# Diagonal sums of five groups by TensorE, loads limited by bytes, and a new order of instructions

## The chip, the cores and the metric

The kernel runs on one core of a Trainium2 chip. Its time is that of one execution on the device in microseconds (us). Five engines work side by side, each through its own queue in the order in which the program gives it instructions: TensorE (PE, with its weight loads as PEld), VectorE (DVE), ScalarE (ACT), GpSimd (POOL) and SyncE (SP). DMAs are issued by SP and at the beginning by ACT; q1 is SP's DMA queue, q8 brings instructions.

## The reference

A linear attention with a decayed state feeds a gated feed-forward layer. Shapes are B=4, H=8 heads, S=768 steps, D=48; x has 384 features, the hidden layer 1024.

```python
for t in range(S):
    kt, vt, rt = k[:, :, t], v[:, :, t], r[:, :, t]
    cur = einsum('bhd,bhe->bhde', u * kt, vt)
    y[:, :, t] = einsum('bhd,bhde->bhe', rt, state + cur)
    state = w * state + einsum('bhd,bhe->bhde', kt, vt)
x = y.transpose(0, 2, 1, 3).reshape(B, S, H * D)
h = maximum(x @ w_in, 0)
conv = conv_w[0] * h[t - 1] + conv_w[1] * h[t] + conv_w[2] * h[t + 1]
out = (h * sigmoid(conv)) @ w_out
```

The current step enters y with u in place of the state: its share is (sum over d of r·u·k) times v, a sum on the diagonal of the score matrix.

## The kernel before, in words

**Attention.** Time is cut into 24 groups of 128 steps (six for each batch row), each of two chunks of 64. A group's data lie in four rotating buffers: KR (k and r with features on the partitions, two DMAs for the two halves of the partitions), and TOK (k, r and v with time on the partitions; `ldT` is its load of k and r, `ldV` that of v). `prep(g)` readies group g: VectorE multiplies KR by powers of the decay (`KR`), GpSimd scales k by tokens (`KS`), and the diagonal of the scores is made. For the first `NE` = 2 groups this diagonal comes from a product k·r with features on the partitions (`P`), 16 TensorE products with one column each (`pq`), and a VectorE multiply with an identity (`dg`); for all others from token products on GpSimd (`KRT`, `KRU`), a reduction on VectorE (`QQ`) and the diagonal on GpSimd (`dg`, in `diagonal`). From group `GP` = 5 on a ScalarE copy (`TKc`) puts the powers into the scores' bank before the multiply.

`visit(g)` is one TensorE stretch: the outputs of group g (bank AV), and the scores (bank SP, key "SUs") and state update (bank UP) of group g+1. Behind it a VectorE copy under a mask (`msk`) adds the scores to the diagonal of group g+1 in SC, and the state goes forward by a multiply (`M`, MM) and an addition (`SA`, SS). For group 2 a visit is cut in two (outputs, then scores). Visit -1 makes only group 0's scores. The outputs go to XF (first three groups) or XT (split into two fp32r parts), and small DMAs (`mv`) move rows of x between partitions.

**Feed-forward.** x is worked through in seven units of columns with eight blocks f of hidden features each. `first` (f1) makes one block in HP0 or HP1, followed by relu, convolution, sigmoid and product in ACT and DVE (HP, CV) and, from unit 1 on, a split into two parts (`GH`, `GL`); `second` (f2) adds up the output in PO0 to PO2. Unit 0 works in fp32. The weights come in 16 pieces of 384 KB; `convert` unpacks a piece with two ACT steps and a DVE step into WF, and `split` makes its two fp32r parts, the high one on ACT and the low one on DVE or POOL.

**The order** of the instructions on all engines comes from the class `Plan`: each step has a cost and a due time, a list of random changes to the due times (`MOVES`: a seed, a share, a size, a place in time) shifts them, and `order` picks at each point the earliest possible and most urgent step. Where it believes TensorE idle ahead of the first f2 it adds a product of 512 columns into PO0 that nobody reads, a fill. Loads of the classes in `LONG` wait for earlier ones: no more than `LOADS` = 6 in flight, and `LATER` = 4 after the first `FIRST` = 40. The loads of groups 4 to 7 also wait for a gate, the mask copy of the group two before.

```python
lim = min(max(f, ready[i]) for i in av) + DELTA
i = min((late[i] - (BON if e == "pe" and ops[i][5] == mode else 0.0), i) for i in av if ready[i] <= lim)[1]
```

## Time and profile before

| | us |
|---|---|
| median of three runs | 302.86 |
| lowest, highest | 302.4, 304.26 |
| the profiled execution | 304.27 |
| its span in the trace | 302.5 |
| TensorE busy | 287.7 (95%) |
| VectorE busy | 222.5 (74%) |
| ScalarE busy | 176.4 (58%) |
| GpSimd busy | 166.2 (55%) |

The span runs from the first to the last instruction of the trace; the execution's own time holds what lies around it. Busy shares are means over the whole span. A visit shows in the trace as lines L638 (scores), L647 and L654 (outputs) and L651 (state); L641 and L644 belong to group 2 alone. f1 is L741, f2 is L788 in unit 0 and L791 later; L874 is a fill. L373 is the helper `tt` for all tensor products on DVE and POOL, which are told apart by their tiles.

### The profile page before, as it was taken

To read this page: it belongs to the slowest core of one execution; us is meant where nothing else is said; L and a number is where in the kernel's file an instruction comes from. 1 tells how busy PE (TensorE), PEld (TensorE's weight loads), DVE (VectorE), ACT (ScalarE), POOL (GpSimd) and SP (SyncE) were. 2 spreads that over 40 slices of the span, in tenths; PEclk is the share of its full clock that TensorE was granted. 3 is DMA by queue.
4 is the path that set the end of the run, shared out by engine and by line. 5 is a ranking of instruction groups with operands and counts; after the bars stand their busy time and mean duration, and the time that the engine had idled before them with its cause. 6 is when DMAs were issued, how large, how long until landed. Compare 5 with 4: busy or idle time off the path is not lost.

```text
span 302.5 us, 9831 instructions
## 1 busy us (share of the span) xinstructions
PE 287.7 (95%) x4104; PEld 239.2 (79%) x4110; DVE 222.5 (74%) x359; ACT 176.4 (58%) x348; POOL 166.2 (55%) x196
## 2 busy tenths in 40 slices
PE   7979999869998999999999999999999999999994
PEld 2657666546777888889888888888888988899993
DVE  5766579896998876877879984899867755556561
ACT  3135484857776456664656753667735665556663
POOL 8367686984678884787735846658511111131230
PEclk9997999998999999999999999999999999999999
DMA  6994695855655535646424453554210020001102
GB/s 155 226 240 130 201 278 158 243 166 158 187 176 154 148 106 146 178 119 172 141 75 126 114 179 64 133 139 143 75 49 14 15 96 7 9 0 62 33 0 78
DMA packets 24011, 37.00 MB, mean 122 GB/s; under 512 B 6256, under 2 KB 16784, under 8 KB 23968
## 3 DMA queue, kind: packets, MB, share of 16 engines
q1 hardware_dynamic: 23632, 36.04, 42.7%
q8 instruction: 32, 0.52, 0.7%
q10 hardware_dynamic: 336, 0.35, 0.5%
q14 instruction: 11, 0.09, 0.1%
HBM read 29.49 MB, written 4.72 MB: 113 GB/s over the span
## 4 chain that ended last, share of the span: by engine, by line
PE 67%; DMA 6%; DVE 5%; POOL 4%; issue 3%; SPq 2%; ACT 2%; POOLq 0%; DVEq 0%; ACTq 0%
PE HP L741 29%; PE PO L791 25%; PE SP L638 4%; POOL TOK L373 3%; PE AV L654 3%; PE PO L788 3%; DMA TOK<-in_krt_dram 2%; PE AV L647 2%; SPq L382 2%; PE UP L651 2%; DMA KR<-in_krd_dram 1%; DMA ST<-in_w_in_dram 1%; DVE CV L753 1%; DVE KR L373 1%; DMA XF<-XF 1%
## 5 line engine op out<-in xcount | busy, mean ns | idle before, releaser
L741 PE MATMUL HP<-XT,wi 128*128 128x464 f32 (+2 forms) x432 | 98.8, 373 | 0.2 <-DVE CV L757 0.2
L791 PE MATMUL PO<-GG,wo 128*128 128x462 f32 (+2 forms) x432 | 97.5, 369 | 0.7 <-POOL GG L763 0.7
L753 DVE SCALAR_TENSOR_TENSOR CV<-HP,cw,CV 128x462 f32<-128x462 f32 (+2 forms) x112 | 75.2, 672 | 21.2 <-ACT CV L750 19.9
L791 PEld LDWEIGHTS PO<-GG,wo 128*128 128x128 f32 x432 | 80.2, 189 | 9.7 <-POOL GG L763 0.9
L741 PEld LDWEIGHTS HP<-XT,wi 128*128 128x128 f32 x432 | 79.5, 189 | 9.6 <-issue 0.4
L763 POOL TENSOR_TENSOR GG<-CV,GG 128x462 fp32r<-128x462 f32 (+2 forms) x30 | 34.7, 1156 | 65.6 <-ACT GG L762 61.0
L749 ACT ACTIVATE HP<-HP 128x464 f32<-128x464 f32 (+2 forms) x56 | 29.3, 523 | 50.4 <-PE HP L741 50.3
L638 PE MATMUL SP<-KR 48*64 48x64 f32 x768 | 46.3, 233 | 5.6 <-DVE KR L373 4.1
L757 DVE TENSOR_TENSOR CV<-HP,CV 128x462 f32<-128x462 f32 (+2 forms) x56 | 34.3, 612 | 21.3 <-ACT CV L756 21.0
L638 PEld LDWEIGHTS SP<-KR 48*64 48x64 f32 x768 | 38.9, 137 | 12.2 <-DVE KR L373 5.9
L654 PE MATMUL AV<-SC,TOK 64*48 64x64 f32 x760 | 47.0, 223 | 0.0
L647 PE MATMUL AV<-KR,SS 48*48 48x64 f32 x696 | 43.8, 223 | 0.0
L756 ACT ACTIVATE CV<-CV 128x462 f32<-128x462 f32 (+2 forms) x56 | 31.9, 569 | 19.8 <-DVE CV L753 19.6
L651 PE MATMUL UP<-TOK 64*48 64x48 f32 x704 | 41.3, 209 | 2.2 <-DVE SS L373 2.2
L750 ACT ACTIVATE CV<-HP,cw 128x462 f32<-128x462 f32 (+2 forms) x56 | 35.1, 627 | 2.3 <-ACT HP L749 0.4
L651 PEld LDWEIGHTS UP<-TOK 64*48 64x48 f32 x704 | 34.1, 127 | 2.3 <-DVE SS L373 2.3
L654 PEld LDWEIGHTS AV<-SC,TOK 64*48 64x48 f32 x760 | 35.7, 124 | 0.0
L647 PEld LDWEIGHTS AV<-KR,SS 48*48 48x48 f32 x696 | 32.5, 123 | 2.0 <-issue 2.0
L373 POOL TENSOR_TENSOR SC<-eye,QQ 128x512 f32<-128x512 f32 x22 | 23.4, 1064 | 18.0 <-PE AV L654 14.2
L762 ACT CAST GG<-CV 128x462 fp32r<-128x462 f32 (+2 forms) x48 | 27.2, 566 | 9.5 <-DVE CV L757 9.1
L373 POOL TENSOR_TENSOR TOK<-TOK 128x384 f32<-128x384 f32 x22 | 22.6, 1027 | 17.9 <-DMA TOK<-in_krt_dram 17.9
L373 POOL TENSOR_TENSOR MM<-SS,w 112x192 f32<-112x192 f32 x36 | 19.0, 528 | 17.1 <-DVE SS L373 15.7
(85 smaller groups left out, 358.8 us busy)
## 6 DMA issues: line engine op xcount, KB each, us to landing
KR<-in_krd_dram SPq DMA_DIRECT2D x46, 192.0 KB, 4.1
TOK<-in_krt_dram SPq DMA_DIRECT2D x22, 384.0 KB, 4.4
TOK<-in_vt_dram SPq DMA_DIRECT2D x47, 96.0 KB, 3.5
ST<-in_w_in_dram SPq DMA_DIRECT2D x8, 384.0 KB, 3.8
ST<-in_w_out_dram SPq DMA_DIRECT2D x8, 384.0 KB, 3.8
XT<-XT SPq DMA_DIRECT2D x126, 16.0 KB, 2.0
...
```

Of the source, the lines that this page charges most:

```text
L373: op(eng, d, rd, wr, lambda e: e.tensor_tensor(**kw), cls, port=not psum)
L638: PE.matmul(SP_[xs[x], p, c], KK[j][rows[x], p, t], RR[j][rows[x], p, t], start=True, stop=True)
L647: PE.matmul(outs[x], state(2 * g + c)[rows[x], p], RR[i][rows[x], p, t], start=not direct, stop=False)
L651: PE.matmul(UP[rows[x], n:n + D], TOK[j][xs[x], 0, p, c], TOK[j][xs[x], 2, p, c], start=True, stop=True)
L654: PE.matmul(outs[x], TOK[i][xs[x], 2, p, c], SC[g % 2][xs[x], p, c], start=none and not direct, stop=True)
L741: PE.matmul(hp[:, at:at + n_], WF[f][:, 0, j * 128:j * 128 + 128] if full else wi[a][:, j, fs], XF[:, j, c0:c0 + w] if full else src(x, j, y),
L750: op("act", act(n, 0, 1), [H_, "cw"], [("T", ti)], lambda e: A.activation(t1, hp[:, 1:n + 1], AF.Copy, scale=cw[:, 3 * f + 1:3 * f + 2]), ...
L753: op("dve", dve(n, psum=1) + 0.02, [H_, "cw"], [("T", ti)], lambda e, k=k: V.scalar_tensor_tensor(out=t1, in0=hp[:, k:n + k], scalar=cw[:, ...
L756: op("act", act(n, 1), [], [("T", ti)], lambda e: A.activation(t1, t1, AF.Sigmoid), "SG")
L757: op("dve", dve(n), [H_], [("T", ti)], lambda e: V.tensor_tensor(out=t1, in0=hp[:, 1:n + 1], in1=t1, op=ALU.mult), "GG")
L763: op("any", {"dve": dve(n), "pool": pool(n, "GL")}, [("T", ti), ("GH", gi)], [("GL", gi)], lambda e: e.tensor_tensor(out=gg(gi)[:, 1, :n], ...
L791: PE.matmul(po[:, :n], wo[a][:, f, ms], gg(gi)[:, x, :n], start=f == 0 and j == 0, stop=f == NF - 1 and j == 2)
```

## The change

Five groups instead of two (`NE`) take their diagonal from TensorE. `pq` is written anew: the product k·r moves through the array (128 columns for each head), and the factor u·w is the stationary operand, spread over 64 columns, so the sum comes out already repeated in 64 rows. That makes eight products instead of 16, and an output of a whole bank. Groups 0 to 2 use HP0, HP1 and PO1; groups 3 and 4 use the scores' bank SP itself. `pks` (scaled k of group 0) moves to PO1. The diagonal step of these groups is the VectorE multiply, and `P` of groups 2 to 4 may go to VectorE or GpSimd. The load of r by tokens for groups 2 to 4 falls away. Loads are no longer counted: their sizes (1.3 for 384 KB of TOK, 0.63 for a half of KR, 0.3 for one of v, 1.28 for a weight piece) may add up to `WAY` = 6.0 in flight. The planner's model of loading code changes, and `MOVES` has a new list of numbers, so everything is in another order.

```diff
-LONG, LOADS = ('ldK', 'ldT', 'ldV', 'wdma'), 6
-NE = 2
+LONG, WAY = ('ldK', 'ldT', 'ldV', 'wdma'), 6.0
+NE = 5
...
-FBASE, FETCH, FIRST, LATER = 3.4, 0.7, 40, 4
+FBASE, FETCH = 3.4, 0.8
...
 MOVES = [
-    (982228, 0.4, 3.0, 105.0), (679522, 0.004, 3.0, 75.0), (769013, 0.03, 1.0, 105.0), (831907, 0.03, 3.0, 45.0),
...
+    (5566, 0.1, 3.0, 105.0), (905251, 0.03, 1.0, 60.0), (855037, 0.1, 8.0, 45.0), (191337, 0.4, 3.0, 0.0),
...
                 if cls in LONG:
-                    k = LOADS if len(loads) < FIRST else LATER
-                    if len(loads) >= k:
-                        tc.add_manual_dep(i.ins, loads[-k].ins.name, behind_, reason="loads")
-                    loads.append(i)
+                    k, way = len(loads), x
+                    while k and way <= WAY:
+                        k -= 1
+                        way += loads[k][1]
+                    if way > WAY:
+                        tc.add_manual_dep(i.ins, loads[k][0].ins.name, behind_, reason="loads")
+                    loads.append((i, x))
...
         def bank(g):
-            return [(HP[0], ("HP", 0)), (HP[1], ("HP", 1)), (PO[1], ("PO", 1))][g] if g < 3 else (UP, "UPq")
+            return [(HP[0], ("HP", 0)), (HP[1], ("HP", 1)), (PO[1], ("PO", 1))][g] if g < 3 else (SP_.rearrange("q p c t -> q (p c t)"), "SUs")
...
-                tt("dve" if g < 3 else ANY, 512, kr(i), [("SC", g % 2)], "P", out=pp, in0=KK[i][0:112], in1=RR[i][0:112], op=ALU.mult)
+                tt("dve" if g < 2 else "any", 512, kr(i), [("SC", g % 2)], "P", out=pp, in0=KK[i][0:112], in1=RR[i][0:112], op=ALU.mult)
...
                 def mq(e):
-                    for c in range(2):
-                        for p in range(NP):
-                            for x in range(2):
-                                r = slice(64 * x, 64 * x + D)
-                                n = NP * 2 * D + p * 2 + c
-                                PE.matmul(kb[64 * x:64 * x + C, n:n + 1], s[r, p, c], uw[r, p:p + 1], start=True, stop=True)
+                    for p in range(NP):
+                        for x in range(2):
+                            r = slice(64 * x, 64 * x + D)
+                            PE.matmul(kb[64 * x:64 * x + C, p * GT:(p + 1) * GT], uw[r, p:p + 1].broadcast_to([D, C]), s[r, p].rearrange("q c t -> q (c t)"), start=True, stop=True)
...
-                op("pe", 1.1, [("SC", g % 2), "uw"], [key], mq, "pq", 1200, mode=1, k=32)
-                q = kb[:, NP * 2 * D:NP * 2 * D + H]
-                if g < 3:
-                    op("dve", dve(512, psum=1), [key, "eye"], [("SC", g % 2)], lambda e: V.tensor_tensor(
-                        out=s.rearrange("q p c t -> q (p c) t"), in0=eye.unsqueeze(1).broadcast_to([128, 2 * NP, C]), in1=q.unsqueeze(2).broadcast_to([128, 2 * NP, C]), op=ALU.mult), "dg")
-                    return
-                op("act", 0.2, [key], [("QQ", g % 2)], lambda e: A.copy(QQ[g % 2], q), "qc")
-                diagonal(g)
+                op("pe", 0.95, [("SC", g % 2), "uw"], [key], mq, "pq", 2100, mode=1, k=16)
+                op("dve", dve(512, psum=1), [key, "eye"], [("SC", g % 2)], lambda e: V.tensor_tensor(
+                    out=s.rearrange("q p c t -> q (p c) t"), in0=eye.unsqueeze(1).broadcast_to([128, 2 * NP, C]), in1=kb.rearrange("q (n t) -> q n t", t=C), op=ALU.mult), "dg")
                 return
```

The order moves at three places of which the prediction speaks. The first is TensorE's queue ahead of visit 3, which begins with the scores of group 4 (KR0_61) and the outputs of group 3 (KR3_64); before:

```order
L874 LDWEIGHTS wz_102
L874 MATMUL PO0_127<-wz_102 128x512
L741 MATMUL HP0_125<-XF_80,WF0_89 128x384 x3
L741 MATMUL HP1_126<-XF_80,WF1_90 128x384 x3
L638 MATMUL SP_122<-KR0_61 64x64 x2
L647 MATMUL AV_124<-KR3_64,SS2_73 48x64 x2
L651 MATMUL UP_123<-TOK0_65 48x48 x2
L654 MATMUL AV_124<-SC1_70,TOK3_68 48x64 x2
```

and now, from the end of visit 2 on (L664 is its last state product, L591 the products for the diagonal of group 4):

```order
L664 MATMUL UP_123<-TOK3_68 48x48 x2
L754 MATMUL HP0_125<-XF_80,WF0_89 128x384 x3
L754 MATMUL HP1_126<-XF_80,WF1_90 128x384 x3
L591 MATMUL SP_122<-SC0_69,uw_106 64x128 x8
L651 MATMUL SP_122<-KR0_61 64x64 x2
L660 MATMUL AV_124<-KR3_64,SS2_73 48x64 x2
L664 MATMUL UP_123<-TOK0_65 48x48 x2
L667 MATMUL AV_124<-SC1_70,TOK3_68 48x64 x2
```

The fills ahead of the first f1 are gone, and eight products into the scores' bank stand between the second f1 and visit 3.

The second is VectorE around visit 1, which needs the state additions SS3 and SS0. Before (KR3_64 is group 3, L659 a mask copy, L509 a weight or convolution piece):

```order
L509 SCALAR_TENSOR_TENSOR WF0_89<-ST1_100 128x384
L373 TENSOR_TENSOR SS3_74<-MM0_75,UP_123 112x192
L659 COPY_PREDICATED SC1_70<-mask_107,SP_122 128x512
L373 TENSOR_TENSOR KR3_64<-KR3_64,PO2_129 112x1024
L373 TENSOR_TENSOR SS0_71<-MM1_76,UP_123 112x192
L509 SCALAR_TENSOR_TENSOR ST0_99<-ST0_99 128x24
L509 SCALAR_TENSOR_TENSOR WF1_90<-ST2_101 128x384
```

and now (L672 is the mask copy, L528 a piece, L598 the diagonal of group 2):

```order
L528 SCALAR_TENSOR_TENSOR ST0_99<-ST0_99 128x24
L672 COPY_PREDICATED SC1_70<-mask_107,SP_122 128x512
L389 TENSOR_TENSOR SS3_74<-MM0_75,UP_123 112x192
L389 TENSOR_TENSOR MM1_76<-SS3_74,w64_112 112x192
L528 SCALAR_TENSOR_TENSOR WF1_90<-ST2_101 128x384
L389 TENSOR_TENSOR SS0_71<-MM1_76,UP_123 112x192
L598 TENSOR_TENSOR SC0_69<-eye_109,PO1_128 128x512
L389 TENSOR_TENSOR KR3_64<-KR3_64,PO2_129 112x1024
L389 TENSOR_TENSOR wi1_118<-WF1_90,wi0_117 128x3x128
L672 COPY_PREDICATED SC0_69<-mask_107,SP_122 128x512
```

The addition SS0 stood behind group 3's multiply and stands now ahead of it, behind the second w_in piece (WF1); the low half of that piece (wi1) comes ahead of group 2's mask.

The third is VectorE ahead of visit 6, which needs group 7 (KR3_64 again). Before:

```order
L753 SCALAR_TENSOR_TENSOR CV4_88<-HP0_125,cw_121,CV4_88 128x382
L659 COPY_PREDICATED SC0_69<-mask_107,SP_122 128x512
L509 SCALAR_TENSOR_TENSOR WF6_95<-ST2_101 128x384
L373 TENSOR_TENSOR SS2_73<-MM1_76,UP_123 112x192
L373 TENSOR_TENSOR KR3_64<-KR3_64,SP_122 112x1024
L757 TENSOR_TENSOR CV4_88<-HP0_125,CV4_88 128x382
```

and now:

```order
L672 COPY_PREDICATED SC0_69<-mask_107,SP_122 128x512
L389 TENSOR_TENSOR XT_79<-AV_124,XT_79 112x4x128
L389 TENSOR_TENSOR SS2_73<-MM1_76,UP_123 112x192
L389 TENSOR_TENSOR KR3_64<-KR3_64,SP_122 112x1024
L766 SCALAR_TENSOR_TENSOR CV4_88<-HP0_125,cw_121,CV4_88 128x382
L528 SCALAR_TENSOR_TENSOR WF6_95<-ST2_101 128x384
```

The piece WF6 stood ahead of the addition and the multiply and stands now behind them.

## Rows read from the trace of the kernel before

**Rows 1.** Windows by stage: length, busy us (instructions), granted clock, DMA share, GB/s.

```profile
23.00:26.40 3.40, 3.17 (x120) 3.17 (x120) 2.00 (x3) 2.14 (x6) 2.43 (x3) 0.52 0.28 83
28.40:33.00 4.60, 4.59 (x161) 4.50 (x162) 1.38 (x3) 2.10 (x6) 2.22 (x4) 1.00 0.64 200
67.40:70.80 3.40, 3.40 (x66) 2.39 (x58) 3.04 (x5) 1.89 (x4) 2.55 (x3) 0.52 0.71 202
92.60:94.10 1.50, 0.02 (x1) 0.00 (x0) 0.74 (x2) 0.59 (x1) 1.50 (x2) 1.00 0.61 204
94.20:292.50 198.30, 198.11 (x2591) 176.99 (x2591) 146.37 (x233) 119.44 (x223) 98.01 (x106) 1.00 0.33 92
```

**Rows 2.** Timeline of PE: start, duration, instruction, idle time before and releaser.

```profile
16.13 0.25 PE L638 MATMUL SP<-KR 48*64 48x64 f32 x2
...
18.23 2.54 PE L874 MATMUL PO<-wz 128*128 128x512 bf16 x11 [0.16 <-issue]
...
23.23 0.32 PE L651 MATMUL UP<-TOK 64*48 64x48 f32 x2 [2.21 <-DVE SS L373]
...
35.52 4.04 PE L741 MATMUL HP<-XF,WF 128*128 128x384 f32 x12
39.49 0.27 PE L638 MATMUL SP<-KR 48*64 48x64 f32 x2
...
46.53 0.27 PE L638 MATMUL SP<-KR 48*64 48x64 f32 x2 [0.39 <-DVE KR L373]
...
57.54 0.28 PE L638 MATMUL SP<-KR 48*64 48x64 f32 x2 [1.03 <-DVE KR L373]
...
66.31 0.33 PE L638 MATMUL SP<-KR 48*64 48x64 f32 x4 [2.66 <-DVE KR L373]
```

**Rows 3.** Timeline of DVE: product, diagonal, multiply of group 3, addition behind it.

```profile
8.30 0.69 DVE L373 TENSOR_TENSOR SC<-KR 112x512 f32<-112x512 f32 x1
...
10.80 0.68 DVE L582 TENSOR_TENSOR SC<-eye,HP 128x512 f32<-128x512 f32 x1
...
21.69 1.22 DVE L373 TENSOR_TENSOR KR<-KR,PO 112x1024 f32<-112x1024 f32 x1 [1.08 <-DMA KR<-in_krd_dram]
22.83 0.35 DVE L373 TENSOR_TENSOR SS<-MM,UP 112x192 f32<-112x192 f32 x1
```

**Rows 4.** The chain of waits, 27 to 36 us: start, us, what.

```profile
30.89 4.16 DMA KR<-in_krd_dram
```

**Rows 5.** Timeline of DVE, 56 to 66 us.

```profile
56.26 1.22 DVE L373 TENSOR_TENSOR KR<-KR,SP 112x1024 f32<-112x1024 f32 x1 [1.06 <-ACT SP L551]
57.40 0.55 DVE L509 SCALAR_TENSOR_TENSOR WF<-ST 128x384 int32<-128x384 int32 x1
...
62.19 2.67 DVE L509 SCALAR_TENSOR_TENSOR WF<-ST 128x384 int32<-128x384 int32 x1
```

**Rows 6.** Timeline of PE: the one-column products, then visit 2's products.

```profile
9.17 1.09 PE L573 MATMUL HP<-uw,SC 48*64 48x1 f32 x32
...
28.61 0.28 PE L644 MATMUL AV<-KR,SZ 48*64 48x64 f32 x4
28.73 0.28 PE L647 MATMUL AV<-KR,SS 48*48 48x64 f32 x4
```

**Rows 7.** Timeline of POOL: scaled k of group 1, diagonal of group 4, token product.

```profile
14.29 0.99 POOL L373 TENSOR_TENSOR TOK<-TOK,TH 128x384 f32<-128x384 f32 x1 [0.70 <-ACT TH L486]
...
41.30 1.04 POOL L373 TENSOR_TENSOR SC<-eye,QQ 128x512 f32<-128x512 f32 x1
...
62.50 0.99 POOL L373 TENSOR_TENSOR TOK<-TOK,TH 128x384 f32<-128x384 f32 x1
```

**Rows 8.** Timeline of ACT: a step of a weight piece.

```profile
23.35 0.55 ACT L504 ACTIVATE ST<-ST 128x384 f32<-128x384 f32 x1
```

**Rows 9.** Timeline of SP: the last move into XF.

```profile
31.52 0.51 SPq L382 DMA_DIRECT2D XF<-XF  x1
```

**Rows 10.** DMA issues, 0 to 75 us: count, KB each, median us to landing.

```profile
XF<-XF SPq DMA_DIRECT2D x3, 16.0 KB, 4.1
```

More of the change, by code (lines that the diff above doesn't have):

```diff
@@ L61 @@
 FN, FE, FW = 512, 6000, 3.4
-FBASE, FETCH, FIRST, LATER = 3.4, 0.7, 40, 4
+FBASE, FETCH = 3.4, 0.8
 GATED = 4
+DIRECT, ACTQ = (2,), (1,)
 DIRECT, ACTQ = (2,), (1,)
@@ L190, in fetched @@
                 at_ = max(s, s + (len(there) - 0.4 - a) * d, there[-1])
-                there.append(at_ + FBASE + FETCH * sum(1 for z in large[-8:] if z > at_))
+                there.append(at_ + FBASE + FETCH * max(0.0, dq - at_ - 0.9))
             for b in range(1, len(there)):
@@ L276, in order @@
                 if cls in LONG:
-                    large.append(done)
+                    large.append((done, x))
             else:
@@ L385, in issue @@
                 if cls in LONG:
-                    k = LOADS if len(loads) < FIRST else LATER
-                    if len(loads) >= k:
-                        tc.add_manual_dep(i.ins, loads[-k].ins.name, behind_, reason="loads")
-                    loads.append(i)
+                    k, way = len(loads), x
+                    while k and way <= WAY:
+                        k -= 1
+                        way += loads[k][1]
+                    if way > WAY:
+                        tc.add_manual_dep(i.ins, loads[k][0].ins.name, behind_, reason="loads")
+                    loads.append((i, x))
             op(q, dur, rd, wr, issue, cls, x, dma=True, gate=gate)
@@ L574, in prep @@
                 if g < NK:
-                    op("pe", 1.1, [k for k in kr(i) if k[0] == "KK"] + ["D64"], [key], mm, "pks", 1700, mode=1, k=32)
-                    op("act", act(384), [key], [("tK", i)], lambda e: A.copy(k_t.rearrange("q p c d -> q (p c d)"), kb[:, 0:NP * 2 * D]), "KSc")
+                    op("pe", 1.1, [k for k in kr(i) if k[0] == "KK"] + ["D64"], [kkey], mm, "pks", 1700, mode=1, k=32)
+                    op("act", act(384), [kkey], [("tK", i)], lambda e: A.copy(k_t.rearrange("q p c d -> q (p c d)"), ks[:, 0:NP * 2 * D]), "KSc")
```

10 lines of the change are left out of this document (7 added, 3 removed), and 49 rows, old and new, of the table MOVES.

## The prediction

> **What bounds the kernel now.** First I read the page's busy time: TensorE is busy for 287.7 of 302.5 us (the table above). The windows by stage say where the rest is [rows 1]: from 94.2 to 292.5 us TensorE is busy for 198.11 of 198.30 us at the full granted clock, so a us won before 94 is a us won at the end, and in that stretch a faster VectorE or GpSimd wins nothing. All that can be won lies ahead, and there it has three forms. TensorE runs fills, products into a bank that nobody reads (52 in the program; eleven took 2.54 us, 0.23 each [rows 2]); it stands still (2.21 us inside visit 1, 0.39, 1.03 and 2.66 us before visits 4, 5 and 6, each put down to VectorE [rows 2], and 1.5 us at 92.6 with no releaser [rows 1]); and twice the granted clock falls to half, 0.52 over 23.0 to 26.4 and over 67.4 to 70.8 us, just behind the two longest stops [rows 1]. A full TensorE loses 3.4 x (1 - 0.52) = 1.6 us in each.
>
> Then I followed each stop to its cause. Visit 1 waits for a state addition that stands on VectorE behind the multiply of group 3; this multiply waited 1.08 us for its load, and the addition ran only at 22.83 [rows 3]. Visit 3 starts at 39.49 [rows 2] behind the chain load of KR for group 4 (landed 30.89 + 4.16 = 35.05 [rows 4]), multiply, and GpSimd's token products. Visit 6 waits because a VectorE conversion, normally 0.55 us, took 2.67 us [rows 5] beside two GpSimd products, the first at 62.50 [rows 7], with the addition and the multiply of group 7 queued behind it.
>
> **The change part by part.** *The products.* Groups 0 and 1 had 16 one-column products, 1.09 us [rows 6]. Now groups 0 to 4 have eight of 128 columns. The trace of before has none; in visit 2 each set of two products of 64 columns on both row halves starts 0.12 us after the last one [rows 6], so 128 columns are 0.24 and four such sets 0.95 us. That lies near the 1.09 of the same helper, and I take 0.95; if the halves don't overlap it is 1.9. Groups 0 and 1 win 0.1 each; groups 2, 3 and 4 add 0.95 each. For 2 and 3 they replace fills (the program has 28 instead of 52) and cost nothing; for group 4 they stand bare between the second f1 and visit 3.
>
> *Diagonals.* Off GpSimd go two token products of 1.0 us and one diagonal of 1.04 us for each of groups 2, 3 and 4 [rows 7], 9.1 us in all; off VectorE goes the reduction. Added are a product on VectorE (0.69) or GpSimd (between 1.04 and 1.33, its 1.00 for 384 columns scaled to 512) and a VectorE diagonal of 0.68 [rows 3]. For groups 3 and 4 the products land in the scores' bank: the mask of the group before must have read it, and visit 3's score products wait until the diagonal of group 4 is out. That is a new stop of 0.68 plus two hand-overs, 0.9 us; VectorE's next item there is free to go, TensorE's queue holds visit 3 and everything behind it, and nothing hides it.
>
> *Loads.* Groups 2 to 4 load only k by tokens, 192 KB less each. Both orders move 3,640 KB up to the end of group 3's KR, so this multiply comes no earlier; what is gained is one more w_in piece among them and, up to group 4's last piece, 576 KB. The limit changes from six (later four) loads in flight to 6.0 units, some 1.8 MB; in the opening the queue is full either way, later loads wait for free buffers first.
>
> *The order, walked with the durations of before.* Visit 0 waited for the one-column products; now these come before the TH products, so it starts when k is scaled, 14.29 + 0.99 = 15.3 [rows 7] instead of 16.13 [rows 2]. TensorE then reaches visit 1 at 15.3 + 1.95 + six fills 1.4 + 0.95 = 19.6. Its state addition now stands ahead of group 3's multiply, but behind the conversion of the second w_in piece. That piece ends at 2,968 KB; in proportion to 3,640 KB at 21.7 us [rows 3] it lands at about 18; four ScalarE steps of 0.55 [rows 8], the conversion of 0.55 and the addition of 0.35 give 21.4. So the stop shrinks from 2.2 to 1.8 us. After 2.2 us the clock fell [rows 1, 2], after the 1.5 at 92.6 it did not [rows 1]; I let it fall here as before, so that visit 1 ends at 25.0 rather than 26.7. If it doesn't, 1.6 us more is won.
>
> Behind it the mask of group 2 (0.7) opens the gate of group 4's loads at 25.7. Both KR halves are now issued straight behind the gate, the second at 26.4 instead of 30.89, and land at 30.5 instead of 35.05 [rows 4]. SyncE's last move of x columns was issued at 31.52 [rows 9] and such a move takes 4.1 us [rows 10], which is 35.6 and sets the first f1 at 35.52 [rows 2]. Now it follows the KR halves at 28.0 and lands at 32.1. Visit 2, with group 3's products ahead of it, (28.4 to 33.0, full throughout [rows 1]) runs from 26.8 to 31.4, so the first f1 starts at 32.1. Two f1 take 4.04 [rows 2], group 4's products 0.95, the diagonal 0.9: visit 3 starts at 37.9, **1.6 us** earlier.
>
> From there the PE order is the same. Before visit 4 the 0.39 us goes, because the diagonal of group 4 is no longer the last of GpSimd's row of 1 us products; one fill more takes 0.23 back: **0.2**. Before visit 5 the multiply waited 1.06 us for a ScalarE copy [rows 5], which stood behind the conversion of a weight piece; that copy now stands behind f1 work only, and the 1.03 goes: **1.0**. Before visit 6 the conversion that took 2.67 us now stands behind the multiply of group 7: **2.7**, and with the stop the half-clock stretch, **1.6**. Together 7.1 us. By hand one sees the waits that go, not the new ones: the four stops of VectorE have a mean of 1.57 us [rows 2], and I give one such back. What is left is 5.5 us.
>
> The tail stays: TensorE now has three products more behind the last f1, but that f1's own chain sets the end, as before; 0 to 0.5 us.
>
> One page speaks against a step of this. The Trainium skill, SBUF — State Buffer, section Who interferes with whom, says that a VectorE instruction with two SBUF inputs and a GpSimd instruction that reads SBUF block one another for whole instructions; the trace agrees (2.67 us for 0.55 [rows 5]). The new order has such a VectorE step, the low half of the second w_in piece, ahead of group 2's mask while GpSimd forms group 3's product. By that rule the gate opens up to 2.1 us later and the gain would be 3.4, 299.5 us.
>
> **The sum.** The profiled execution took 304.27 us for a span of 302.5, so 1.8 lies around it, and 298.8 would be its time with the change. The median of the three runs is 302.86, 1.4 below. I set the gain against it: 302.86 - 5.5 = **297.4 us**. If the 1.4 of that execution is among what goes, the time is 298.8.
>
> **The rivals.** *A, the waits move instead of going.* The opening is bound by loads, and 3,640 KB stand ahead of the same multiply in both. Then visits 4 to 6 find new late loads, and only the 1.6 of visit 3 stays: 301.3. For it: visit 1's stop is a load's. Against it: the last two stops are queue order, not bytes.
>
> *B, slower: the scores' bank as a chain.* From KR of group 4 to visit 3 there are now multiply, mask, product, TensorE, diagonal in series, where GpSimd worked beside TensorE. If KR lands later than about 33 us (before: 35.05 [rows 4]), visit 3 starts at 35.52 + 4.04 + 0.95 + 0.9 = 41.4, 1.9 later than before, and with a stop as long as those that dropped the clock 1.6 more: 302.86 + 3.5 = 306.4. Against it: the gate opens earlier even with a slow visit 1.
>
> *C, the clock.* With 24 fills fewer there are waits where fills stood, and two more stretches at half clock cost 3.3: 300.7. For it: both stretches of before follow a stop [rows 1]; against it, the fills that went are replaced by products mostly.
>
> *D, deeper queues.* With 1.8 MB in flight the x moves and code loading wait longer; three stops like that at 92.6 us (1.5 [rows 1]) cost 4.5: 301.9. The Trainium skill, DMA: Bandwidth & Descriptors, section Queues, rings and completion order, says that a DMA engine takes its queue rows in turn by packets; by that rule code loading, which has its own queue, pays nothing for a deeper load queue. No row here shows it.
>
> **How the numbers follow.** Forecast 0.60, A 0.15, B 0.09, C 0.10, D 0.06. The whole 7.1, visit 1 at full clock (1.6) and the stop at 92.6 gone (1.5) give 302.86 - 10.2 = 292.7; the range is 293.0 to 303.0, which holds most of the forecast, A, C and D (0.8) and leaves out B. A measurement of this kernel can tell about 1%, 3.0 us, from no change. Faster by more: nearly all of the forecast, a fifth of A, a third of C and a quarter of D, 0.67. Slower by more: two thirds of B and a little of D, 0.07. The rest, 0.26, is within 1%.
>
> **What would show it.** Eight-column-block products of 0.95 us a group; VectorE's reduction first seen at group 5; visit 1's stop under 2 us; KR of group 4 landing near 30.5; the first f1 near 32 and visit 3 near 38 with a stop of 0.9 ahead of it; no stop over 1 us before visits 5 and 6; one half-clock stretch at most. The prediction is wrong if KR of group 4 lands after 33, if a products' group takes 1.9, or if stops appear after 94 us.

## The result: no gain, and the profile after

| | kernel before | changed kernel |
|---|---|---|
| median on the same chip, 20 runs each | 301.59 us | 304.82 us |
| lowest and highest | 299.64, 304.26 (and one of 714.75) | 301.30, 309.19 |
| the profiled execution | 304.27 | 306.57 |
| its span | 302.5 | 304.8 |

The ratio of the times is 1.0061, with a 95% interval of 1.0038 to 1.0084: at most 1% slower, where 297.4 us had been forecast. (The ratio leaves out executions more than 1.5% above the fastest of their kernel, nine of the changed kernel's 20 and its profiled one among them; that of the medians is 1.011.)

To see where the time went, the span is cut at the same places of the program in both kernels: start of visit 0, the first f1, visits 5, 7 and 8, end. The windows of the kernel before, with length, busy time and instructions of TensorE, of its weight loads, of VectorE, ScalarE and GpSimd, then granted clock, DMA share and GB/s:

```profile
16.13:35.52 19.39, 16.71 (x435) 12.74 (x435) 12.27 (x21) 9.53 (x25) 12.25 (x15) 0.91 0.65 181
35.52:57.54 22.02, 20.11 (x289) 12.64 (x289) 18.47 (x30) 14.52 (x31) 18.16 (x19) 1.00 0.77 223
57.54:81.56 24.02, 21.36 (x291) 14.27 (x291) 20.64 (x33) 16.50 (x37) 17.30 (x18) 0.93 0.60 178
81.56:90.76 9.20, 9.20 (x160) 7.48 (x159) 9.14 (x13) 6.79 (x15) 5.79 (x8) 1.00 0.63 179
90.76:302.50 211.74, 206.06 (x2736) 183.65 (x2735) 151.72 (x243) 125.45 (x236) 102.52 (x110) 1.00 0.33 92
```

and of the changed kernel:

```profile
16.00:30.46 14.46, 12.81 (x443) 10.58 (x444) 11.68 (x22) 8.96 (x23) 7.70 (x8) 1.00 0.70 192
30.46:56.33 25.87, 21.82 (x309) 13.68 (x307) 23.58 (x33) 14.84 (x32) 15.49 (x17) 1.00 0.71 200
56.33:78.73 22.40, 19.25 (x287) 12.32 (x288) 20.06 (x30) 14.44 (x32) 16.03 (x18) 1.00 0.64 169
78.73:88.56 9.83, 9.83 (x161) 7.66 (x160) 8.43 (x14) 7.24 (x15) 7.60 (x8) 1.00 1.05 229
88.56:304.80 216.24, 208.92 (x2739) 185.83 (x2738) 155.08 (x250) 124.23 (x237) 94.71 (x103) 0.98 0.31 88
```

Read the first columns against each other: -4.9 us up to the first f1, +3.9 to visit 5, -1.6 to visit 7, +0.6 to visit 8, +4.5 from there to the end; with 0.1 won at visit 0 that is +2.3, the difference of the spans. So a gain is made, up to the first f1 more than forecast, and given back, above all at two places: between the first f1 and visit 5, and behind visit 8.

The places show in the timeline of TensorE of the changed kernel (start, duration, instruction, idle time before and releaser; L754 is f1, L591 the new products, L651, L664 and L667 belong to visits, L801 is f2):

```profile
30.46 0.91 PE L754 MATMUL HP<-XF,WF 128*128 128x384 f32 x2
34.53 1.09 PE L591 MATMUL SP<-SC,uw 48*64 48x128 f32 x16
36.41 0.27 PE L651 MATMUL SP<-KR 48*64 48x64 f32 x2 [0.79 <-DVE SC L598]
42.78 0.27 PE L651 MATMUL SP<-KR 48*64 48x64 f32 x2
52.02 2.19 PE L801 MATMUL PO<-CV,WF 128*128 128x382 f32 x6 [0.98 <-DVE WF L528]
56.33 0.27 PE L651 MATMUL SP<-KR 48*64 48x64 f32 x2 [2.11 <-DVE KR L389]
63.08 0.25 PE L664 MATMUL UP<-TOK 64*48 64x48 f32 x2 [0.38 <-DMA ST<-in_w_in_dram]
66.86 2.21 PE L754 MATMUL HP<-XF,WF 128*128 128x384 f32 x6 [1.96 <-DVE CV L770]
94.19 0.45 PE L667 MATMUL AV<-SC,TOK 64*48 64x64 f32 x3 [3.66 <-issue]
```

Against [rows 2]: the first f1 is 5.1 us earlier, visit 3 3.1, visit 4 3.75; visit 5, after stops of 0.98 and 2.11, only 1.2. Behind those stops stands one VectorE instruction, in the timeline of VectorE:

```profile
45.31 6.66 DVE L528 SCALAR_TENSOR_TENSOR WF<-ST 128x384 int32<-128x384 int32 x1
51.89 0.34 DVE L389 TENSOR_TENSOR SS<-MM,UP 112x192 f32<-112x192 f32 x1
```

and at the same time on GpSimd:

```profile
44.79 0.99 POOL L389 TENSOR_TENSOR TOK<-TOK 128x384 f32<-128x384 f32 x1
45.75 1.03 POOL L389 TENSOR_TENSOR SC<-eye,QQ 128x512 f32<-128x512 f32 x1
46.75 0.98 POOL L389 TENSOR_TENSOR TOK<-TOK 128x384 f32<-128x384 f32 x1
47.71 1.94 POOL L389 TENSOR_TENSOR TOK<-TOK,TH 128x384 f32<-128x384 f32 x2
49.61 1.94 POOL L389 TENSOR_TENSOR TOK<-TOK,uu 128x384 f32<-128x384 f32 x2
56.88 1.43 POOL L389 TENSOR_TENSOR SC<-eye,QQ 128x512 f32<-128x512 f32 x1 [5.33 <-DVE QQ L605]
```

A conversion of a weight piece, 0.55 us elsewhere [rows 5], lasts 6.66 us and ends 0.4 us after GpSimd's unbroken run does, whose last seven steps go from 44.79 to 51.55. A later conversion is held beside GpSimd's products up to 65.4, and the f1 at 66.86 waits:

```profile
62.12 3.70 DVE L528 SCALAR_TENSOR_TENSOR WF<-ST 128x384 int32<-128x384 int32 x1
```

Not every conversion beside GpSimd is held. The one before, in the same unbroken run, took 0.58 us, and here it was GpSimd's next step that took longer (0.83 us, where the same product takes 0.51 at 59.65):

```profile
43.89 0.58 DVE L528 SCALAR_TENSOR_TENSOR WF<-ST 128x384 int32<-128x384 int32 x1
44.00 0.83 POOL L389 TENSOR_TENSOR MM<-SS,w 112x192 f32<-112x192 f32 x1
```

The other place, in windows of the changed kernel:

```profile
86.00:90.53 4.53, 4.53 (x138) 3.82 (x136) 3.90 (x8) 2.47 (x5) 4.51 (x7) 1.00 1.02 199
90.53:94.19 3.66, 0.00 (x1) 0.00 (x1) 0.61 (x2) 0.00 (x0) 1.66 (x2) 0.81 0.38 112
94.20:97.70 3.50, 3.50 (x11) 2.97 (x12) 2.40 (x5) 1.93 (x4) 1.89 (x2) 0.50 0.40 126
97.70:101.00 3.30, 3.30 (x13) 2.86 (x13) 0.62 (x2) 1.40 (x3) 1.73 (x3) 0.71 0.09 20
101.00:292.50 191.50, 191.50 (x2548) 170.57 (x2547) 145.12 (x232) 113.90 (x216) 87.46 (x94) 1.00 0.32 90
```

The last products of visit 8 come after a stop of 3.66 us in which no engine releases anything, where the kernel before stood 1.50 us [rows 1]. Ahead of it the DMA engines are fully busy; behind it the granted clock is 0.50 for 3.5 us and 0.71 in the mean of the next 3.3, which costs another 3.5 x 0.50 + 3.3 x 0.29 = 2.7 us. From 101 us on TensorE is full as before.

### The profile page after: what moved, and what is told of

Read it like the earlier page. It is cut to its first block, busy times and chain, and to the rows that moved or that the text cites. A ratio compares the mean times of both kernels' runs of the same rounds, so it can differ in the third digit from the quotient of the medians.

```text
span 304.8 us, 9798 instructions
## 1 busy us (share of the span) xinstructions
PE 286.1 (94%) x4098; PEld 238.1 (78%) x4102; DVE 229.7 (75%) x370; ACT 174.5 (57%) x348; POOL 149.6 (49%) x179
## 4 chain that ended last, share of the span: by engine, by line
PE 82%; DVE 7%; issue 3%; DMA 3%; POOL 2%; ACT 2%; SPq 0%; ACTq 0%; POOLq 0%
PE HP L754 33%; PE PO L804 29%; PE SP L651 6%; PE AV L667 4%; DVE WF L528 4%; PE AV L660 3%; PE UP L664 3%; PE PO L801 2%; DMA uc<-in_ut_dram 2%; DVE CV L766 2%; DMA TOK<-in_krt_dram 1%; POOL SC L389 1%; ACT CV L763 1%; PE PO L887 1%; DVE CV L770 1%
## 5 line engine op out<-in xcount | busy, mean ns | idle before, releaser
L754 PE MATMUL HP<-XT,wi 128*128 128x464 f32 (+2 forms) x432 | 100.4, 377 | 0.0
L804 PE MATMUL PO<-GG,wo 128*128 128x462 f32 (+2 forms) x432 | 98.8, 371 | 0.4 <-ACT GG L775 0.3
L754 PEld LDWEIGHTS HP<-XT,wi 128*128 128x128 f32 x432 | 81.0, 191 | 9.8
L776 POOL TENSOR_TENSOR GG<-CV,GG 128x462 fp32r<-128x462 f32 (+2 forms) x24 | 28.2, 1174 | 59.0 <-ACT GG L775 56.7
L770 DVE TENSOR_TENSOR CV<-HP,CV 128x462 f32<-128x462 f32 (+2 forms) x56 | 34.3, 612 | 23.4 <-ACT CV L769 22.9
L667 PE MATMUL AV<-SC,TOK 64*48 64x64 f32 x760 | 45.3, 217 | 3.7 <-issue 3.7
L651 PE MATMUL SP<-KR 48*64 48x64 f32 x768 | 44.7, 228 | 2.9 <-DVE KR L389 2.1
L651 PEld LDWEIGHTS SP<-KR 48*64 48x64 f32 x768 | 37.8, 133 | 10.6 <-issue 3.8
L660 PE MATMUL AV<-KR,SS 48*48 48x64 f32 x696 | 42.0, 217 | 0.0
L664 PE MATMUL UP<-TOK 64*48 64x48 f32 x704 | 39.8, 204 | 0.9 <-issue 0.5
L667 PEld LDWEIGHTS AV<-SC,TOK 64*48 64x48 f32 x760 | 34.5, 119 | 3.8 <-issue 3.8
L389 POOL TENSOR_TENSOR SC<-eye,QQ 128x512 f32<-128x512 f32 x19 | 20.2, 1064 | 34.4 <-PE AV L667 28.3
L664 PEld LDWEIGHTS UP<-TOK 64*48 64x48 f32 x704 | 33.1, 122 | 1.2 <-issue 0.6
L389 POOL TENSOR_TENSOR TOK<-TOK,TH 128x384 f32<-128x384 f32 x23 | 24.7, 1079 | 1.5 <-ACT TH L505 1.0
```

The lines of the kernel that those rows point to most:

```text
L389: op(eng, d, rd, wr, lambda e: e.tensor_tensor(**kw), cls, port=not psum)
L651: PE.matmul(SP_[xs[x], p, c], KK[j][rows[x], p, t], RR[j][rows[x], p, t], start=True, stop=True)
L660: PE.matmul(outs[x], state(2 * g + c)[rows[x], p], RR[i][rows[x], p, t], start=not direct, stop=False)
L664: PE.matmul(UP[rows[x], n:n + D], TOK[j][xs[x], 0, p, c], TOK[j][xs[x], 2, p, c], start=True, stop=True)
L667: PE.matmul(outs[x], TOK[i][xs[x], 2, p, c], SC[g % 2][xs[x], p, c], start=none and not direct, stop=True)
L754: PE.matmul(hp[:, at:at + n_], WF[f][:, 0, j * 128:j * 128 + 128] if full else wi[a][:, j, fs], XF[:, j, c0:c0 + w] if full else src(x, j, y),
```

## The experiments

**The theory.** Two losses hide the gain: the held conversion, and TensorE out of instructions inside visit 8, because the DMA that brings the next piece of its program waits behind the burst of loads. The rivals: the new products and VectorE's diagonals set the waits; the loads themselves are the limit, so that any wait taken away comes back; the byte limit alone makes the queue too deep. Each kernel was timed in 3 rounds with the kernel before on the same chip, whose median lay between 301.2 and 301.7 us; ratios are to it.

### The held conversion

Three kernels keep the changed kernel's order and add waits on GpSimd; the numbers are steps of the program, the one ahead of the colon waits for the one behind it:

```diff
+PORT = {427: 224, 293: 297}   # a_wait
+PORT = {235: 228, 293: 297}   # a_port
+PORT = {306: 228}             # a_dose
...
 made[i] = plan.ops[i][3](eng[place[i]])
+if i in PORT:
+    tc.add_manual_dep(made[i].ins, made[PORT[i]].ins.name, behind_, reason="port")
```

**a_wait.** 

> The changed kernel with two waits added on GpSimd: its product on the KRT tokens that ran beside VectorE's conversion WF of group 4 (6.66 us at 45.31, where the same conversion takes 0.55 us elsewhere) waits until that conversion is done, and the one beside the conversion WF of group 6 (3.70 us at 62.12) likewise. Order and all else unchanged. Theory (VectorE's conversion is held while GpSimd runs, and visit 5 and the f1 before visit 7 pay for it): both conversions take under 1 us, the wait of 2.11 us before visit 5 falls under 0.5, the waits of 0.98 (f2) and 1.96 us (f1 at 66.86) go, visit 8 begins 4 to 5 us before 88.56; the time is 3 to 5 us under the changed kernel's 304.8, if the half clock behind visit 8 stays as it is. Rival (the new products on TensorE or the later loads set these waits): the conversions may shorten, but visits 5 and 7 stay within 0.5 us of 56.33 and 78.73, and the time stays at 304 to 306. Second rival: GpSimd, made to wait, is late itself for visit 6, whose wait then grows from 0.38 to over 1.5 us.

Measured: 304.01 us, ratio 1.0002 (0.9961 to 1.0043), from 299.1 to 309.5. The first wait was put on the conversion one place ahead (step 224 for 228) and does nothing: 6.65 us as before, and the stops of 0.96 and 2.11 stay. The second one works (0.77 instead of 3.70) and the wait before that f1 goes. But waits of 0.70 and 1.26 us for later conversions, themselves behind w_out pieces that had not landed, take its place, and visit 7 begins 48.5 us after the first f1, where it was 48.3. So the first half is not tested here, and in the second the loads are the next limit.

**a_port.** 

> The changed kernel with two waits added on GpSimd, now on the conversion that was held: the mask of the diagonal (SC from eye and QQ, 45.75) waits for VectorE's conversion WF that took 6.66 us from 45.31, and the product wo at 62.49 for the conversion that took 3.70 us from 62.12. Order and all else unchanged. Theory (GpSimd's unbroken run holds the conversion, and TensorE pays 2.11 and 0.98 us for it): both conversions take 1.6 us or less, the waits ahead of visit 5 and of the f2 before it fall to under 0.5 us together, and visit 5 begins 23 to 24 us after the first f1 instead of 25.9. What becomes of it: if nothing else is late, visit 8 begins 54 to 56 us after the first f1 instead of 58.1 and the time is 301 to 303. Rival (loads are the next limit, as the wait before the f1 at 66.86 came back further on when the second of the two waits alone was effective): visit 5 is earlier, but waits on landed w_out pieces or conversions of 2 us or more stand ahead of visits 6 and 7, visit 8 begins 57.5 us or more after the first f1, and the time is 304 to 306.

Measured: 301.53 us, ratio 1.0016 (0.9986 to 1.0047), where the changed kernel has 1.0061: some 1.4 us less by the ratios, whose intervals still touch (the medians differ by 3.3). The conversion in the timeline of VectorE of a_port:

```profile
46.45 0.89 DVE L529 SCALAR_TENSOR_TENSOR WF<-ST 128x384 int32<-128x384 int32 x1
```

beside it GpSimd:

```profile
45.93 0.99 POOL L390 TENSOR_TENSOR TOK<-TOK 128x384 f32<-128x384 f32 x1
47.48 1.04 POOL L390 TENSOR_TENSOR SC<-eye,QQ 128x512 f32<-128x512 f32 x1 [0.56 <-DVE WF L529]
```

and visit 5 on TensorE:

```profile
54.04 0.27 PE L652 MATMUL SP<-KR 48*64 48x64 f32 x2
```

A wait of 0.56 us on GpSimd wins 5.8 us on VectorE. Visit 5 has no stop ahead and begins 22.4 us after the first f1 (31.60) instead of 25.9; visit 8 53.5 after it instead of 58.1, at 85.05. The theory holds here and the rival of the loads falls.

**a_dose.** 

> The changed kernel with one wait on GpSimd, three instructions further into its unbroken run: the product on KRU that began at 49.61 waits for VectorE's conversion WF that took 6.66 us from 45.31. Theory (a conversion with two SBUF inputs, caught beside GpSimd, ends only when GpSimd's run pauses): it ends within 0.5 us of the end of the instruction before the wait, so it takes 4 to 5 us, between the 6.66 without a wait and the 0.9 with the wait on the first instruction; the waits ahead of the f2 and of visit 5 (0.98 and 2.11) come to 0.5 to 1.5 us together, and the time is 302.5 to 304.5. Rival (one GpSimd instruction holds it, and 6.66 us came from something else): the conversion takes under 2 us or still 6 to 7.

Measured: 302.99 us, ratio 1.0017 (0.9982 to 1.0052). The conversion in the timeline of VectorE of a_dose:

```profile
46.80 4.76 DVE L529 SCALAR_TENSOR_TENSOR WF<-ST 128x384 int32<-128x384 int32 x1
```

and GpSimd beside it:

```profile
49.20 1.95 POOL L390 TENSOR_TENSOR TOK<-TOK,TH 128x384 f32<-128x384 f32 x2
51.64 1.00 POOL L390 TENSOR_TENSOR TOK<-TOK,uu 128x384 f32<-128x384 f32 x1 [0.49 <-DVE WF L529]
```

GpSimd pauses at 51.15, the conversion ends at 51.56. With a pause after the first instruction of the run, after the fifth, and only at its end after the seventh, it takes 0.89, 4.76 and 6.66 us, and the stops ahead of visit 5 come to 0, 1.46 and 3.09. That a pause releases it is shown; why this conversion is caught and the one before it is not stays open.

### The stop inside visit 8

**a_count.** 

```diff
-while k and way <= WAY:
...
+k = 6 if len(loads) < 40 else 4
+if len(loads) >= k:
+    tc.add_manual_dep(i.ins, loads[-k][0].ins.name, behind_, reason="loads")
```

> The changed kernel with the loads limited by their number again (6 in flight, 4 after the first 40), as in the kernel before; order and all else unchanged. Theory (a deep load queue holds back the transfer that brings TensorE's next instructions, so that TensorE runs out of them at 90.53 for 3.66 us and then runs at half clock): the stop inside visit 8 is 1.5 us or less, as in the kernel before, no stretch between 94 and 101 us has a granted clock under 0.9, and the time is 3 to 5 us under 304.8. Rival (the limit by bytes was what brought group 4's tokens earlier and nothing else): the stop stays near 3.66 us, and the x transfers queued behind waiting loads make visits 3 to 5 later by 1 us or more; the time is 305 or more.

Measured: 311.38 us, ratio 1.0332 (1.0270 to 1.0395). The stop is still 2.96 us. Waits for conversions (1.99 us before an f2) are new, since the order was made for the other limit. As to the limit the theory falls.

**b_bytes.** The same exchange the other way round, in the kernel before and its order.

> The kernel before, in its own order, with the loads limited by bytes as in the changed kernel and nothing else. Theory (the deep load queue is what lengthens the stop inside visit 8): the stop at 92.6 grows from 1.5 to 3 us or more and the clock falls behind it; against that, group 4's KR tokens land before 35.05 and the first f1 comes up to 3 us earlier; together 301 to 305 against 301.6. Rival (the stop has nothing to do with the loads): it stays at 1.5 us, no half clock behind it, and only the gain of the earlier tokens is left, 299 to 301.

Measured: 301.55 us, ratio 1.0010 (0.9976 to 1.0044). Visit 8 has no stop at all, which neither expectation had; in the windows of b_bytes:

```profile
89.32:91.58 2.26, 2.26 (x130) 2.08 (x129) 2.06 (x4) 1.51 (x4) 1.93 (x2) 1.00 0.78 235
```

So the byte limit costs nothing, and it is the new order, which issues 15 loads between 75 and 87 us with no x move among them, that fills the queues: 1.05 against 0.63 of the DMA engines' time in the windows from visit 7 to visit 8 above.

**a_shift.** 

```diff
-PE.matmul(PO[0][:, :FN], wz[:, :128], wz[:, :FN], start=True, stop=True)
+for h in range(2):
+    PE.matmul(PO[0][:, 256 * h:256 * h + 256], wz[:, :128], wz[:, 256 * h:256 * h + 256], start=True, stop=True)
```

> The changed kernel with each of the 512-column products on zeros (those ahead of the first visit) issued as two of 256 columns: the same columns, 38 more pairs of weight load and product, so that the places in TensorE's instructions at which a further piece of them has to arrive fall elsewhere. Theory (the stop of 3.66 us inside visit 8 is TensorE out of instructions): the stop moves by some 70 instructions to an earlier place or goes, since the piece is asked for earlier, when fewer loads are queued; without it and the half clock behind it the time is 3.5 to 7 us under 304.8, and at worst the same with the stop at another time. Rival (the stop belongs to the data or the place in visit 8): it stays at the same product of visit 8, 3 to 4 us long, and the time stays within 1 us of 304.8.

Measured: 305.40 us, ratio 1.0147 (1.0115 to 1.0180). Visit 8 runs through (2.04 us), no half clock follows, and from its start to the last product take 208.8 us instead of 213.0: the theory's sign. The time misses what was expected, because the finer fills brought four stops of 0.5 to 1.0 us without a releaser ahead of the first f1, which starts at 33.45 instead of 30.46. So the shift has to come later.

**a_split.** 

```diff
+if full and f < 4:
+    h = (n + 2) // 2
+    for o in (0, h):
+        for j in range(3):
+            PE.matmul(hp[:, o:o + h], WF[f][:, 0, j * 128:j * 128 + 128], XF[:, j, c0 + o:c0 + o + h], start=j == 0, stop=j == 2)
+    return
```

> The changed kernel with the first four blocks' products f1 on WF (three of 384 columns each, from 30.5 us on) issued as six of 192 columns: the same columns, 12 more products, all after the visits 0 to 2, so that only later pieces of TensorE's instructions are cut elsewhere. Theory (the 3.66 us inside visit 8 is TensorE out of instructions because the next piece was asked for only as the visit began): the stop goes or falls under 0.5 us, no stretch after it is at half clock, from visit 8's start to the end take about 209 us instead of 213, and the time is 300 to 302. Rival (the stop comes from the place or the state of the queue, whatever the cut): it stays at 3 us or more, the half clock behind it too, and the time is 304 to 306. Second rival: the narrower products cost TensorE time of their own, 1 us or more before 45 us.

Measured: 303.38 us, ratio 1.0039 (1.0001 to 1.0077). Visit 8 in the windows of a_split, with the DMA engines 0.90 busy:

```profile
91.44:93.47 2.03, 2.03 (x130) 1.95 (x129) 1.30 (x3) 1.14 (x3) 2.03 (x3) 1.00 0.90 208
```

No stop; 207.3 us from there to the last product. The whole does not reach 300 to 302, because visit 5 and the f1 behind visit 6 still wait 2.12 us each for held conversions, and behind the second wait the clock falls (0.67 from 67.9 to 73.0 us).

**a_hold.** 

```diff
+lim = 2.0 if 62 <= k < 76 else WAY
-while k and way <= WAY:
+while k and way <= lim:
...
-if way > WAY:
+if way > lim:
```

> The changed kernel with the 14 loads issued from 77 to 100 us limited to a third of the bytes in flight, the earlier and later ones as they were; TensorE's instructions unchanged. Theory (the instruction piece waits behind the queued loads): it is under way within 1 us of visit 8's start instead of 3.2, the stop is 1.7 us or less instead of 3.66, and the time 301 to 303.5, the lower if the half clock behind the stop goes too. Rival (the piece is late for another reason, such as when it is asked for): the stop stays at 3 us or more, and the time at 304 to 306 or above it if the x transfers behind the held loads come late.

Measured: 306.47 us, ratio 1.0164 (1.0118 to 1.0210). The stop in the timeline of TensorE of a_hold, with TensorE's program unchanged:

```profile
88.91 0.31 PE L668 MATMUL AV<-SC,TOK 64*48 64x64 f32 x3 [0.87 <-issue]
```

It is 0.87 us instead of 3.66. The earlier start of visit 8 (86.07) is not the cause: in a_port it starts at 85.05, and the stop is 3.94. The time misses what was expected, because an f2 then waits 3.30 us for ScalarE, which waits for an output buffer, whose DMA stands behind the held loads in SyncE's queue. By chance this execution repeats a_dose: GpSimd waited 0.39 us for tokens that landed late, and the conversion ended there; visit 5 has no stop.

```profile
45.46 1.89 DVE L529 SCALAR_TENSOR_TENSOR WF<-ST 128x384 int32<-128x384 int32 x1
47.32 1.00 POOL L389 TENSOR_TENSOR TOK<-TOK 128x384 f32<-128x384 f32 x1 [0.39 <-DMA TOK<-in_krt_dram]
```

**b_split** and **b_cut.** The half widths of a_split in the kernel before, for four blocks and (`f < 1`) for one.

> The kernel before with the first four f1 blocks in half widths and nothing else: TensorE's instructions are cut elsewhere from 36 us on. Theory (its stop of 1.5 us inside visit 8 is the same want of instructions as in the changed kernel): the stop goes and nothing takes its place, 299.5 to 301 against 301.7. Rival: the stop stays or another visit's end falls on a cut, 301 to 304.

> The kernel before with only the first f1 block in half widths: TensorE's instructions are shifted by a quarter as much as with four blocks, after which the stop stood at the end of visit 7 instead of visit 8. Theory (a stop needs a cut near the end of a visit while loads queue): the cut lies 10 to 15 instructions earlier in visit 8 and well behind visit 7, no stop over 0.6 us in either, 299.5 to 301 against 301.4. Rival (the cut in visit 8 has to go further): a stop of 1 us or more stays there, 301 to 303.

Measured: b_split 303.05 us, ratio 1.0048 (1.0016 to 1.0079). The stop has left visit 8, but one stands at the end of visit 7, the rival's sign. From the windows of b_split:

```profile
78.12:80.07 1.95, 1.95 (x123) 1.83 (x123) 1.95 (x4) 1.45 (x4) 0.23 (x1) 1.00 0.89 187
80.07:83.00 2.93, 0.00 (x1) 0.00 (x0) 1.25 (x3) 0.16 (x1) 1.99 (x2) 1.00 0.31 74
83.00:86.20 3.20, 3.20 (x16) 2.76 (x16) 1.85 (x3) 1.99 (x4) 2.41 (x3) 0.69 0.68 209
```

Twelve products more, the last of them issued 29 us ahead, put a stop of 2.93 us into visit 7 in place of the one of 1.51 in visit 8: it belongs to the program's cut into pieces, not to data. b_cut has no stop in either visit of its profile, but its median is 301.24, ratio 0.9999 (0.9967 to 1.0032); the gain of 1.5 is not seen. That the kernel before does not have its stop in each execution would explain this, but is not shown.

The profiles with a stop in visit 7 or 8, and two without one, together. The piece of the program is one DMA packet of 16 KB in queue q8 (kind "instruction", 32 in a run); the page of the kernel before counts 4,104 products and 4,110 weight loads on TensorE, 257 for each packet, so q8 is read as TensorE's program. The share is that of the load queue q1 in the DMA engines' time in the 4 us ahead of it; for b_split and b_best the visit is 7.

| kernel | visit begins | piece begins, landed | share ahead | stop | TensorE goes on |
|---|---|---|---|---|---|
| before | 90.76 | 91.33, 92.75 | 0.48 | 1.51 | 94.12 |
| changed | 88.56 | 91.78, 92.84 | 0.96 | 3.66 | 94.19 |
| a_count | 91.81 | 93.93, 95.27 | 0.92 | 2.96 | 96.74 |
| a_port | 85.05 | 88.31, 89.34 | 0.95 | 3.94 | 90.96 |
| a_dose | 89.45 | 91.06, 92.14 | 0.99 | 1.93 | 93.35 |
| a_wait | 91.35 | 94.46, 95.81 | 1.04 | 4.08 | 97.40 |
| a_hold | 86.07 | 86.25, 87.17 | 0.41 | 0.87 | 88.91 |
| b_split | 78.12 | 80.57, 81.75 | 0.87 | 2.93 | 83.00 |
| b_best | 78.68 | 79.71, 81.19 | 0.98 | 1.93 | 82.56 |
| b_clear | 89.13 | 89.36, 90.65 | 0.72 | 1.12 | 91.99 |
| b_bytes | 89.32 | 88.80, 89.77 | 0.53 | none | |
| a_split | 91.44 | 89.72, 90.90 | 1.03 | none | |

TensorE goes on 1.2 to 1.7 us after the piece has landed. Six of these runs have the same TensorE program (changed, a_count, a_port, a_dose, a_wait, a_hold), and in all six TensorE stands still ahead of the same instruction, for the same piece, the eleventh. The trace does not show when a piece is asked for; but in a_hold, with the queue at 0.41, it begins 0.18 us into the visit, and in the other five, with 0.92 to 1.04, 1.6 to 3.3 us into it. And with a full queue there is no stop if the cut lies elsewhere (a_split).

### Both together

**a_best**: the waits of a_port and the half widths of a_split. **a_first**: and group 4's products ahead of the second f1:

```diff
 seq, place = plan.order()
+seq = list(seq)
+seq.remove(169)
+seq.insert(seq.index(190), 169)
```

> The changed kernel with both: GpSimd's two waits on the held conversions, and the first four f1 blocks issued in half widths. Theory (two independent losses): 297.5 to 300.5, under both kernels. Rival (the conversions' gain is given back to the loads): as with the halved widths alone, 300 to 302. If the stop in visit 8 has another cause than the cut: 303 or more.

> The changed kernel with both edits (the waits on GpSimd and the half widths, 298.3), and group 4's eight products put ahead of the second f1 instead of behind it. Theory (the 0.79 us stop ahead of visit 3 is the chain of products, mask and visit, which the second f1 can cover): no stop ahead of visit 3, visits 3 to 5 0.6 to 0.8 us earlier against the first f1, 297.4 to 298. Rival (VectorE is late with the mask for its own queue, or the gain is given back at the next wait): the stop stays or visits 5 and 6 begin as before, 298 to 299.

Measured: a_best 298.29 us, ratio 0.9895 (0.9842 to 0.9948); a_first 297.79 us, ratio 0.9881 (0.9838 to 0.9924). Both, with four executions each, are faster than both kernels: the ratios lie 1.0 and 1.2% under the kernel before and 1.7 and 1.8% under the changed one's 1.0061, which is 5.0 and 5.4 us. The granted clock is 1.00 over the whole of either profile. The timeline of TensorE in a_first:

```profile
30.89 2.22 PE L754 MATMUL HP<-XF,WF 128*128 128x192 f32 x12
33.04 1.09 PE L592 MATMUL SP<-SC,uw 48*64 48x128 f32 x16
34.06 2.22 PE L754 MATMUL HP<-XF,WF 128*128 128x192 f32 x12
```

The stop before visit 3 (at 36.21, 5.3 us after the first f1 instead of 5.95) is gone; but an f1 then waits 0.46 and visit 4 0.33, and visit 5 begins 22.9 us after the first f1, where it was 22.5 in a_best. Of the 0.79 us nothing is left at visit 5, and the two medians cannot be told apart.

**b_best** and **b_clear.** The counterparts in the kernel before: the wait for step 300 on GpSimd's step 355, with four half-width blocks and with one.

> The kernel before with half widths and a wait on GpSimd, so that both kernels can be compared without the two losses: the product KS at 62.5 waits for VectorE's conversion WF of 62.19 (2.67 us). Theory (visit 6's wait of 2.66 us follows from that conversion as well): the conversion takes under 1 us, visit 6 waits 1 to 1.5 us less, 298 to 300. Rival (visit 6 waits for its tokens' load and GpSimd's chain, not for the conversion): its wait stays over 2.3 us, and the time is that of the half widths alone. If the change itself brings nothing, this kernel and the changed one with the same two edits (298.3) lie within 1 us.

> The kernel before with the first f1 block in half widths and GpSimd's product KS at 62.5 waiting for VectorE's conversion WF of 62.19: no stop for instructions and a shorter wait ahead of visit 6 (1.28 us instead of 2.68 with that wait). Theory: 298 to 300. Compared with the changed kernel cleared of both (298.3): if it is 298.8 or less, the change itself is worth nothing; at 300 to 301 it is worth 2 us, at 303 5 us, as forecast.

Measured: b_best 304.50 us, ratio 1.0106 (1.0071 to 1.0140); b_clear 300.79 us, 0.9994 (0.9962 to 1.0026). In both the conversion is short (0.57 and 0.76 us) and visit 6 waits 1.28 us instead of 2.66; the next f2 then waits 0.85 for a conversion that is held 2.8 to 3.1 us itself. In the time nothing clear is won by it: b_best lies 1.5 us above b_split, b_clear 0.5 under b_cut. b_best has the stop in visit 7, 1.93 us, and the half clock behind it; b_clear still has 1.12 us in visit 8. Neither is wholly clear, then, and b_clear has half widths in one block, a_best in four. Against b_clear a_best is 2.5 us faster, of which 1.1 may be that stop; the intervals of the two ratios leave some 1 to 5 us.

## Why the prediction was wrong

**The step that failed is the term of 1.57 us for new waits, with rival D behind it.** The forecast took five terms of gain, 7.1 us, and gave one mean wait back. What was given back is 0.98 + 2.11 us ahead of visit 5, 1.96 + 0.25 + 0.56 between visits 6 and 7, 3.66 - 1.51 inside visit 8 and 2.7 behind it, 10.7 us in the profile. The mechanism of each was in the text, with a wrong place or size:

- *The held conversion.* It was priced at 2.1 us, at the mask of group 2, where it did not come. "The 1.03 goes" before visit 5 failed: the copy was free of its old neighbour, but the multiply stood behind a conversion held for 6.66 us. "Behind the multiply of group 7: 2.7" held for visit 6 (0.38 us instead of 2.66), and the conversion, 3.70 us there, was paid for by the f1 at 66.86. The Trainium skill, SBUF — State Buffer, section Who interferes with whom, speaks of such instructions blocking one another; the runs agree, and show how long it can last: to the next pause of GpSimd, here after up to seven instructions (a_port, a_dose). The 2.67 us that gave the price were such a rest of a run, too: before, GpSimd's run ends at 64.44 and the conversion of [rows 5] at 64.86, in the timeline of GpSimd:

```profile
63.46 0.98 POOL L373 TENSOR_TENSOR TOK<-TOK,uu 128x384 f32<-128x384 f32 x1
65.20 0.51 POOL L373 TENSOR_TENSOR MM<-SS,w 112x192 f32<-112x192 f32 x1 [0.76 <-DVE SS L373]
```

- *Instructions.* Rival D, at 0.06, priced three stops of 1.5 us; it was one of 3.66, and the half clock, which D left out. The depth that D blamed was not the cause (b_bytes), the burst in the new order was (a_hold). By the Trainium skill, DMA: Bandwidth & Descriptors, section Queues, rings and completion order, a DMA engine takes its queue rows in turn, from which the prediction drew that code loading pays nothing. The runs contradict this conclusion: the piece has a queue of its own and still began 1.6 to 3.3 us into the visit when loads filled the engines, and 0.18 us when they did not (a_hold). The measurement decides; whether the engines take turns as the page says is not shown either way.

**The base.** The 5.5 us were taken from 302.86, the median of three; over 20 it is 301.59. And they were read from an execution with two stretches at half clock, a mean granted clock of 0.989. Of the 76 executions of this kernel timed beside the experiments 9 have a mean that low, 46 have 0.992 to 0.994 and 21 at least 0.998: in most of them one of the two stretches or both were not there to be won.

**What held.** KR of group 4 came sooner, and earlier than forecast (its multiply ran at 28.59). Visit 1 lost neither 1.8 us nor the clock: it was done at 22.83, not 25.0, and the first f1 came at 30.46, not 32.1. (The terms of that sum make 21.1, not 21.4, and a stop of 1.5 us, after which [rows 1] show no fall of the clock.) The products took 1.09 us, as the rows of the same helper had it, not 0.95; the new stop before visit 3 was 0.79 (forecast 0.9). Visit 3 was 3.1 us earlier instead of 1.6, and so rival B, the chain through the scores' bank, did not come. Rivals A and C came in part: the waits did move, and the half clock came behind visit 8. None of the three signs of being wrong came as written (the stop in visit 8 ends at 94.19); the sign that failed is "no stop over 1 us before visits 5 and 6", with 2.11 before visit 5.

**How much is the change's own.** Cleared of both losses it reaches 298.29, close to the 297.4 of the forecast, but that is partly luck: the base was 1.3 us lower than taken, and some of the gain is the kernel before's own loss too. Against the kernel before, nearly cleared (b_clear), it is about 2.5 us, not 5.5. No run separates the new products from the new order; b_bytes shows only that the byte limit alone wins nothing in the old order.

**Open.** The changed kernel's profile is one execution, 1.8 us above its median, and the mean granted clock of the 20 goes from 0.983 to 1.000: the stop and the half clock need not be the same in each. The same program up to 44 us gave 30.46 and 32.89 as the start of the first f1 (changed kernel and a_wait), by stops of 0.4 to 0.9 us without a releaser at other places; whether these are late pieces too was not tried. The changed kernel's 20 executions spread over 7.9 us, the four of a_best over 2.9: that a late token now and then pauses GpSimd, as in a_hold, would make such a spread, but is only argued.
